# States of eleven chunks on ScalarE in eight scaled pieces, sums merged across tiles, Sin tables first, and a new order: one core of a Trainium2 chip

## The chip, the cores and the metric

The kernel runs on one core of one Trainium2 chip. The time is that of one execution on the device, in microseconds (us). A core has five engines that run side by side, each through its own list of instructions in order: TensorE (PE; its weight loads are shown apart as PEld), VectorE (DVE), ScalarE (ACT), GpSimd (POOL) and SyncE (SP), which here only issues transfers. One engine waits for another by semaphores.

## The reference

Two layers in a row, batch 4, 768 positions (S), 8 heads of 48 columns (D), 384 columns together (C). The first is a linear attention with a state that decays:

```python
for t in range(S):
    cur = np.einsum('bhd,bhe->bhde', u[None] * kt, vt)
    y[:, :, t] = np.einsum('bhd,bhde->bhe', rt, state + cur)
    state = wt[:, :, :, None] * state + np.einsum('bhd,bhe->bhde', kt, vt)
```

The second takes the 384 columns of y, projects them to three parts and gates them:

```python
proj = x @ w_proj
x1, x2, x3 = (proj[..., :D].copy(), proj[..., D:2 * D].copy(), proj[..., 2 * D:].copy())
X2 = np.fft.rfft(x2, n=S, axis=1)
H = np.fft.rfft(filter_fft, n=S, axis=0)[None, :, :]
x2_conv = np.fft.irfft(X2 * H, n=S, axis=1)
y = x1 * x2_conv * x3
return (y @ w_out).astype(np.float32)
```

Inputs and output are float32.

## The kernel before, in words

**Attention.** The 768 positions are cut into 6 chunks of 128, so that the 4 batches have 24 chunks, numbered through. For a chunk SP loads w, k, r and v (ldw, ldk, ldr, ldv; 192 KB each, six buffers of each). ACT takes the logarithm of w (lw). PE multiplies it by triangular masks, which gives the sums of logarithms up to each position (cs, and ce without the position itself; ce's last 8 columns are the sums over the whole chunk). ACT's exponentials of these (en or enp, eq) scale k and r (kh or khp, q or qp, on POOL or DVE), PE transposes both (tqk), ACT or DVE copies the result to SBUF (tT), and PE forms the scores (sc), which are masked on DVE (mt), or copied by ACT and masked on POOL (ma, mm). The state is carried by kv on PE: the state of the chunk before, taken in through an identity, plus k times v. Then S scales it by the chunk's decay: in the kernel before that is one VectorE product for every chunk (L610). The output of a chunk is y (or yb, where PE also adds the bonus term vc through an identity; with y, xn on DVE adds it). The bonus needs the row sums of r k u (rk, rku, cc, then vc on POOL). yt transposes y, xT copies it.

**Gate.** After the third chunk of a batch, sums and differences of mirrored chunks are formed (sa, sb) and folded once more (fp, fm), which shortens the Fourier sums. x2 projects them, ab copies, f is the forward transform in six slots, da and db multiply by the filter's transform (UA, UB), pp adds both (P), i1 and i2 are the inverse transform, s and d combine their sum and difference (SD), p1 and p3 are the other two projections (x1, and g or gc with gm), yy multiplies everything, po is the output product, o its copy, st the store. At the end of batch 3 the inverse transform and the gates run in halves (i1h, ech, sh, dh, yyh).

**Start.** POOL makes index ramps and masks, DVE makes angles (ang), ACT takes their sines (F, the transform matrix). The filter is loaded whole (filt, 1152 KB), folded to a sum and a difference (fs, fd: L399, L402), transformed by hf and turned into factors by ht, hr, hb, he.

**What sets the order.** A string, ORDER, written out by hand or by a program, holds one word for each step: the engine's letter (P, V, A, G, S), the step's name, its chunk or batch, and after @ the PSUM bank. Every engine issues its words in that sequence; a "!" makes a POOL step wait for the DVE step of certain kinds that stands last ahead of it. Banks 0 to 5 hold one tile at a time, so that a word with a bank waits until the bank's last reader is done. Each step is a function `op_<name>`; L237 is the line of every copy by ACT, L238 of those by DVE and POOL.

Of the kernel before, what the change touches and what calls it, by code (L numbers as in the profile page):

```python
# [10 lines left out]
FP32 = mybir.dt.float32  # L11
BF16 = mybir.dt.bfloat16
# [25 lines left out]
V:mem1 V:mem3 G:mkd! G:mke! G:iota! V:mem0 A:tLn G:mki! S:ldw1 S:ldu S:ldw0 A:lw1 V:mem4 V:mem2  # L38
A:lw0 G:iorot! P:zs29@0 V:ang2 S:ldr0 S:ldk0 S:ldk1 S:ldw2 S:ldr1 P:cs1@0 A:en1 V:ang1 V:ang0 V:mem7
A:uc0 P:cs0@1 A:en0 S:ldfilt P:ce1@2 S:ldv0 S:ldw3 V:rk0 A:eq1 G:rk1! V:mem5 V:angn G:kh0! P:us0@0  # L40
G:q1! S:ldr2 P:ce0@3 A:uv0 A:sin V:rku0 V:kh1 V:rku1 V:cc0 P:mtr0@0 A:eq0 A:lw2 P:tqk1@2 V:cc1 V:fs
A:tT1 P:ce2@3 P:cs2@1 P:mtr2@4 A:eq2 P:hf0@2 A:mc0 V:q0 V:rsc S:ldk2 A:v0 A:lw3 V:fd G:rk2! G:q2!
A:ht0.1 A:mc2 A:ht0.0 S:ldv1 A:enp2 P:hf1@3 P:tqk0@5 V:mem6 V:ms0 A:tT0 P:kv0@0 V:hr0.1 V:ms2
V:hr0.0 V:S0 P:hf2@2 V:khp2 P:sc0@8 A:he P:cs3@0 A:ht1.1 S:ldk3 S:ldw4 P:tqk2@1 A:ht1.0 V:rku2
G:vc0! G:v1! P:ce3@3 P:hf3@5 S:ldr3 S:ldv2 V:mt0 V:cc2 V:hr1.1 P:yb0@2 A:eq3 P:sc1@8 V:hr1.0 G:vc1!
S:ldw5 A:enp3 A:lw4 S:ldv3 V:mt1 A:tT2 A:v2 A:xc0 G:rk3! G:rku3! P:kv1@3 P:hf4@4 P:cs4@5 G:vc2! V:S1
V:khp3 A:enp4 A:ht2.0 P:yb1@1 P:yt0@2 G:v3! G:q3! P:kv2@3 S:ldk4 S:ldr4 V:cc3 S:ldr5 A:lw5 A:ht2.1
S:ldk5 G:rk4! G:vc3! P:ce4@0 P:sc2@8 P:ce5@4 A:xT0 A:xc1 A:eq5 V:S2 S:ldv4 P:hf5@3 P:tqk3@2 A:eqp4
# [5 lines left out]
P:yt5@1 P:ce7@5 V:sa4 P:x20.0.1@3 V:khp6 A:xT5 A:eq7 V:sb4 P:tqk6@4 V:sa5 A:ab0.0.1 P:x20.1.1@5
V:sb5 V:fp0.0 A:xT3 S:ldr7 A:v6 V:fm0.1 P:x20.0.0@3 P:x20.1.2@2 V:rku6 V:fm0.0 V:fp0.1 S:ldw8 G:q7!
P:x20.0.2@1 S:ldk7 A:ab0.0.0 S:ldp0 A:ab0.1.2 A:ab0.1.1 V:tT6 A:ab0.0.2 S:ldw10 V:cc6 P:f0.0@3
G:kh7! A:xT4 S:ldk8 P:kv6@2 P:x20.1.0@4 V:da0.0 G:vc6! A:ab0.1.0 A:lw8 P:f0.3@1 A:hb2 V:S6 G:rk7!
P:sc6@8 S:ldr8 P:f0.2@4 P:f0.4@2 A:wc0 P:ce8@3 P:tqk7@0 A:eq8 V:db0.1 A:tT7 S:ldw9 P:f0.5@1 P:cs8@5
V:da0.1 V:da0.2 G:rku7! P:p10.2.1@4 V:mt6 G:pp0.1! P:p10.0.1@3 P:p10.2.0@2 A:x10.2.1 S:ldv7 V:db0.2
# [48 lines left out]
A:tT21 G:kh22! V:db2.0 G:kh23! G:v21! A:eqp23 P:f2.5@1 V:qp23 A:ab2.0.0 V:db2.2 P:yb19@2 P:sc21@8
# [844 lines left out]
```

## Time and profile before

| | |
|---|---|
| median of 3 runs | 151.19 us (150.94 to 152.24) |
| the profiled execution | 150.74 us |
| its span, first to last instruction | 148.9 us |
| PE, DVE, ACT, POOL busy | 134.0, 134.8, 130.7, 108.8 us |
| mean granted clock of TensorE | 0.951 of full speed |
| transfers | 27.40 MB in 105702 packets, mean 184 GB/s |

The profile is that of one execution. Busy time is the union of an engine's instructions; neighbours on an engine overlap a little, so the time from one start to the next is shorter than a duration. A row of a timeline has start, duration, engine, line, operation, output and inputs, shape and count, and in brackets the idle time ahead of it with what ended it. A row of a table of stretches has the stretch, its length, then busy time and count for each engine, the granted clock, the share of the transfer engines and GB/s. The chain is the sequence of work that ended last, followed back from the last instruction.

### The profile page before, as it was taken

What the parts mean: (1) busy time and instruction counts of PE and PEld (TensorE: products, weight loads), DVE (VectorE), ACT (ScalarE), POOL (GpSimd) and SP (SyncE); (2) the same over time, 40 slices, a digit from 0 to 9 for tenths busy, and PEclk for the clock granted to TensorE, in tenths of its full rate; (3) what the DMA queues carried; (4) which work ended last, traced back from release to release, by engine and by line L of the source; (5) the groups of instructions that cost most, each with busy time, mean ns of one, the idle gap of its engine ahead of it and who ended that gap; (6) DMA issues with size and microseconds to landing.
All of it is one profiled execution on the core that took longest, in us unless ns stands there. A gap on an engine that the chain in (4) does not pass through costs nothing.

```text
span 148.9 us, 4080 instructions
## 1 busy us (share of the span) xinstructions
PE 134.0 (90%) x1499; PEld 89.9 (60%) x1499; DVE 134.8 (91%) x278; ACT 130.7 (88%) x274; POOL 108.8 (73%) x133
## 2 busy tenths in 40 slices
PE   6625699898999899999999999999999999999990
PEld 6423365666655567777666757666666776555840
DVE  6534999999999999999999999999999999999950
ACT  3799699999999899999999999999999975768470
POOL 7034179995579799999659999695599995846530
PEclk9955559999999999999999999999999999999998
DMA  4998999999999999989999999989980046001854
GB/s 80 212 278 218 181 210 187 219 188 243 178 258 201 263 203 183 217 167 214 227 232 200 222 204 194 198 168 219 229 186 0 4 173 254 0 0 53 314 210 170
DMA packets 105702, 27.40 MB, mean 184 GB/s; under 512 B 100305, under 2 KB 105682, under 8 KB 105682
## 3 DMA queue, kind: packets, MB, share of 16 engines
q1 hardware_dynamic: 105682, 27.14, 81.1%
q8 instruction: 11, 0.18, 0.5%
q14 instruction: 9, 0.07, 0.1%
HBM read 22.41 MB, written 4.72 MB: 182 GB/s over the span
## 4 chain that ended last, share of the span: by engine, by line
PE 68%; DMA 12%; SPq 5%; POOL 4%; DVE 4%; issue 3%; ACT 1%; ACTq 0%; DVEq 0%; POOLq 0%
PE p L688 14%; PE po L852 8%; PE i L773 6%; PE x L719 6%; PE tqk L561 6%; DMA filt<-in_moe_filter_fft_dram 5%; SPq L464 5%; PE sc L574 4%; DMA ldv<-in_v_dram 4%; DMA ldk<-in_k_dram 3%; PE f L739 3%; PE y L627 2%; PE yt L650 2%; PE cs L474 2%; PE kv L602 2%
## 5 line engine op out<-in xcount | busy, mean ns | idle before, releaser
L535 POOL TENSOR_TENSOR rk<-ldr,ldk 128x384 bf16<-128x384 f32 x23 | 23.0, 1003 | 11.1 <-DMA ldr<-in_r_dram 5.6
L688 PE MATMUL p<-xT,wproj 128*128 128x384 bf16 x144 | 28.8, 326 | 0.0
L555 POOL TENSOR_TENSOR vc<-v,cc 128x384 bf16<-128x384 bf16 x24 | 19.9, 831 | 10.5 <-PE sc L574 3.1
L581 DVE TENSOR_TENSOR mt<-sc,mask_excl 128x1024 bf16<-128x1024 f32 x21 | 25.4, 1210 | 0.1
L237 ACT ACTIVATE qkT<-tqk 128x1024 bf16<-128x1024 bf16 x22 | 22.7, 1031 | 0.7 <-PE tqk L561 0.5
L532 POOL TENSOR_TENSOR qk<-ldr,eq 128x384 bf16<-128x384 f32 x20 | 20.1, 1007 | 3.3 <-DVE rku L538 1.8
L561 PE MATMUL tqk<-ident,qk 128*128 128x128 bf16 x192 | 16.2, 228 | 2.6 <-POOL qk L532 1.8
L688 PEld LDWEIGHTS <-wproj 128*128 128x128 bf16 x144 | 13.0, 97 | 7.4 <-ACT wproj L237 0.3
L561 PEld LDWEIGHTS <-qk 128*128 128x128 bf16 x192 | 12.7, 102 | 5.5 <-POOL qk L532 2.2
L470 ACT ACTIVATE lg<-ldw 128x384 bf16<-128x384 f32 x24 | 12.6, 532 | 2.8 <-DMA ldw<-in_w_dram 2.8
L852 PE MATMUL po<-wout,y 128*128 128x384 bf16 x72 | 14.4, 326 | 0.0
L237 ACT ACTIVATE x<-p 128x384 bf16<-128x384 f32 x24 | 11.7, 505 | 1.5 <-PE p L688 1.5
L237 ACT ACTIVATE ab<-x 128x384 bf16<-128x384 f32 x24 | 11.7, 501 | 1.1 <-PE x L719 0.8
L538 POOL TENSOR_TENSOR rku<-rk,u_bc 128x384 bf16<-128x384 bf16 x13 | 11.8, 913 | 0.4
L541 DVE TENSOR_REDUCE cc<-rku 128x8 f32<-128x384 bf16 x22 | 11.7, 537 | 0.0
L499 ACT ACTIVATE eq<-ce 128x392 f32<-128x392 f32 (+1 forms) x21 | 10.6, 514 | 0.6 <-PE ce L486 0.3
L764 DVE TENSOR_TENSOR UB<-f,T 128x768 bf16<-128x768 f32 x12 | 11.1, 943 | 0.0
L237 ACT ACTIVATE v<-ldv 128x384 bf16<-128x384 f32 x20 | 10.8, 548 | 0.3 <-DMA ldv<-in_v_dram 0.2
L237 ACT ACTIVATE xT<-yt 128x384 bf16<-128x384 bf16 x22 | 10.8, 503 | 0.2
L610 DVE TENSOR_TENSOR S<-kv,eq 128x384 bf16<-128x384 f32 x20 | 10.9, 543 | 0.0
L528 POOL TENSOR_TENSOR qk<-ldk,en 128x384 bf16<-128x384 f32 x10 | 10.0, 1003 | 0.8 <-DMA ldk<-in_k_dram 0.8
L761 DVE TENSOR_TENSOR UA<-f,T 128x768 bf16<-128x768 f32 x11 | 10.3, 943 | 0.1
(152 smaller groups left out, 372.9 us busy)
## 6 DMA issues: line engine op xcount, KB each, us to landing
ldw<-in_w_dram SPq DMA_DIRECT2D x24, 192.0 KB, 3.8
ldr<-in_r_dram SPq DMA_DIRECT2D x24, 192.0 KB, 4.2
ldk<-in_k_dram SPq DMA_DIRECT2D x24, 192.0 KB, 3.7
ldv<-in_v_dram SPq DMA_DIRECT2D x24, 192.0 KB, 3.8
out_dram<-o SPq DMA_DIRECT2D x12, 192.0 KB, 2.3
out_dram<-filt SPq DMA_DIRECT2D x12, 192.0 KB, 2.2
o<-in_moe_w_proj_dram SPq DMA_DIRECT2D x3, 576.0 KB, 6.0
filt<-in_moe_filter_fft_dram SPq DMA_DIRECT2D x1, 1152.0 KB, 8.0
```

Source lines behind the costliest of these rows:

```text
L237: return nc.scalar.activation(out=o, in_=i, func=AF.Copy)
L470: nc.scalar.activation(out=lg_b[c % 3][:, :, 0:D], in_=ld["w"][c % LD], func=AF.Ln)
L532: return two(e).tensor_mul(qk_b[c % 3][:, 0, :, 0:D], ld["r"][c % LD], eq)
L535: return two(e).tensor_mul(rk_b[c % 2], ld["r"][c % LD], ld["k"][c % LD])
L538: return two(e).tensor_mul(rku_b[c % 2], rk_b[c % 2], u_bc)
L541: nc.vector.tensor_reduce(out=cc_b[c % 3], in_=rku_b[c % 2], axis=AX.X, op=ALU.add)
L555: return two(e).tensor_mul(vc_b[c % 3], v_b[c % 4], cc_b[c % 3].to_broadcast([L, H, D]))
L561: nc.tensor.transpose(p[:, x, j, :], qk_b[c % 3][:, x, 2 * j:2 * j + 2, :], ident)
L581: nc.vector.tensor_mul(mt_b[c % 3], bank_of[f"sc{c}"].rearrange("p q j t -> p (q j) t"), dataclasses.replace(m[:, :], ap=[m[:, :].ap[0], [ ...
L688: nc.tensor.matmul(p, wproj[:, n, cb, fb * L:(fb + 1) * L], xT_b[b % 2][:, NT * hf:NT * hf + NT, cb, :], start=(cb == 0), stop=(cb == CB - 1),
L764: nc.vector.tensor_mul(UB[:, n], twice(bank_of[f"f.{b}.{2 * n + 1}"][:, :]), t2(n, 1))
L852: nc.tensor.matmul(p, y_b[0][:, cb, ti * L:(ti + 1) * L], wout[:, cb, :], start=(cb == FIRST[0]), stop=(cb == FIRST[-1]),)
```

## The change

**States.** `op_S` gets a second form. Where the word's engine is A, ScalarE makes a chunk's state in eight pieces of 128x48, one for each of the 4 pairs of heads and each head of a pair, since one ACT instruction takes one scale for a partition:

```diff
     def op_S(e, c):
         ph = eq_b[c % 3][:, C:].rearrange("p (a b) -> p a b", b=2)
+        if e == "A":
+            for j in range(HP):
+                for i in (0, 1):
+                    nc.scalar.activation(
+                        out=S_b[nth(c)][:, j, i], in_=bank_of[f"kv{c}"][:, j, i], func=AF.Copy,
+                        scale=ph[:, j, i:i + 1],
+                    )
+            return
         nc.vector.tensor_mul(
             S_b[nth(c)], bank_of[f"kv{c}"], ph.to_broadcast([L, HP, 2, D])
         )
```

The words are A:S0, S1, S2, S4, S7, S8, S9, S10, S15, S19 and S22; the other nine states stay on V.

**Merged steps.** The tiles sd, fo and SD become one tile each, so that one instruction covers what two or three did:

```diff
+    def op_fpm(e, b):
+        return two(e).tensor_add(fo[:, :, 0], sd[:, :, 0], sd[:, :, 2])
+
+    def op_fmm(e, b):
+        return two(e).tensor_sub(fo[:, :, 1], sd[:, :, 0], sd[:, :, 2])
...
+    def op_ppm(e, b):
+        return two(e).tensor_add(P_b[b % 2], UA, UB)
...
+    def op_yym(e, b):
+        return two(e).tensor_mul(y_b[0], SD, g_b[b % 2])
```

fpm and fmm (two 384-wide halves each) take the place of all 16 fp and fm, ppm (2304 wide) of pp in batches 0 and 1, yym (2304 wide) of yy in batches 0 to 2. In batch 3 the last half of one gate is cut in two (yyq).

**Sin first.** The tables for Sin are loaded ahead of everything, the angles follow, then the sines as steps of their own, then the tables for the logarithm and exponential; before, those of the logarithm were first, and Sin lay between:

```diff
-    def op_sin(e, k_):
-        for ti in range(NT):
-            nc.scalar.activation(
-                out=F[:, ti, :], in_=low[:, ti * S:(ti + 1) * S], func=AF.Sin,
-                scale=TWO_PI / UNIT,
-            )
+    def op_tS(e, k_):
+        nc.scalar.preload_act_table(AF.Sin)
...
+    def op_sn(e, ti):
+        nc.scalar.activation(
+            out=F[:, ti, :], in_=low[:, ti * S:(ti + 1) * S], func=AF.Sin,
+            scale=TWO_PI / UNIT,
+        )
```

**Small new steps.** hm, um and uw prepare a tile uh that no step of the new order reads (a mask on POOL, three 8-wide products on PE, one small product on DVE); z2 is two warming products of 512 columns. Further functions (rt, rT, cu, cv, gg, ic, dg and others) are defined and not called.

**Order.** All of ORDER is new. By its words the engines also trade other steps: v leaves ACT for POOL and DVE (20 to 16 on ACT), copies xT go from ACT to DVE (2 to 7 on DVE), the copies of y on ACT go from 15 to 11 (one of them, xr, gets its bonus on POOL by xg), the sums xn on DVE from 9 to 13 and the bonus products on PE (yb) from 15 to 10, three sign copies (ms) go from DVE to ACT, fs goes from DVE to POOL, gc on ACT rises from 6 to 8 and X from 1 to 4. Two lines of it, old and new:

```diff
-V:mem1 V:mem3 G:mkd! G:mke! G:iota! V:mem0 A:tLn G:mki! S:ldw1 S:ldu S:ldw0 A:lw1 V:mem4 V:mem2
+S:ldw1 V:mem1 G:iota0! V:mem7 V:mem0 G:mki! G:mke! G:hm0! G:mkd! S:ldu V:mem5 S:ldw2 A:tS0 S:ldv0
...
```

Three places of the instruction lists show it. First ACT from the program's start; lg is the logarithm of w, cs and en the exponential for k, eq that for r, F the sines. Before:

```order
L342 ACT_TABLE_LOAD
L470 ACTIVATE lg_104<-ldw_80 128x8x48
L470 ACTIVATE lg_103<-ldw_79 128x8x48
L492 ACTIVATE en_110<-cs_267 128x384
L237 ACTIVATE u_top<-u_row 1x384
L492 ACTIVATE en_109<-cs_276 128x384
L499 ACTIVATE eq_113<-ce_280 128x392
L237 ACTIVATE u_bc<-us 128x384
L346 ACT_TABLE_LOAD
L346 ACTIVATE F<-o_170 128x768 x3
L350 ACTIVATE rot<-rang 128x12
L351 ACT_TABLE_LOAD
```

and now:

```order
L362 ACT_TABLE_LOAD
L240 ACTIVATE u_top<-u_row 1x384
L368 ACTIVATE F<-o_171 128x768 x2
L374 ACTIVATE rot<-rang 128x12
L368 ACTIVATE F<-o_171 128x768
L365 ACT_TABLE_LOAD
L493 ACTIVATE lg_105<-ldw_81 128x8x48
L240 ACTIVATE u_bc<-us 128x384
L493 ACTIVATE lg_103<-ldw_79 128x8x48
L493 ACTIVATE lg_104<-ldw_80 128x8x48
L240 ACTIVATE m_b<-mtr_295 128x2x192
L417 ACTIVATE m_b<-mtr_295 128x2x192
```

then, three exponentials further on, the state of chunk 0 (S from kv, eight pieces) up to the logarithm for chunk 4:

```order
L522 ACTIVATE eq_112<-ce_314 128x392
L529 ACTIVATE cs_326<-cs_326 128x384
L648 ACTIVATE S_137<-kv_344,eq_112 128x48 x8
L522 ACTIVATE eq_114<-ce_331 128x392
L493 ACTIVATE lg_104<-ldw_83 128x8x48
```

Two table loads stand where three stood, the sines stand ahead of the first logarithm instead of behind two, and the state of chunk 0 stands between the exponentials of chunks 0 and 2.

Second POOL, around the filter's folded sum (UA from filt, 1152 wide); vc is the bonus term of chunk 0, q and rk those of chunks 2 and 1. In the list before no such row exists on POOL. Now:

```order
L561 TENSOR_TENSOR rku_117<-rk_115,u_bc 128x384
L555 TENSOR_TENSOR qk_106<-ldr_91,eq_112 128x8x48
L590 TENSOR_TENSOR vc_128<-v_121,cc_125 128x384
L422 TENSOR_TENSOR UA<-filt 128x1152
L555 TENSOR_TENSOR qk_108<-ldr_93,eq_114 128x8x48
L558 TENSOR_TENSOR rk_115<-ldr_93,ldk_87 128x384
L558 TENSOR_TENSOR rk_116<-ldr_92,ldk_86 128x384
```

The sum moved here from DVE, ahead of q of chunk 2 and rk of chunks 2 and 1.

Third ACT in the stretch of chunks 7 to 11, in the middle of the program; qkT is the transposed q and k, xT the transposed y, x the first projection, eq, en, cs and ce exponentials, lg logarithms. Before:

```order
L492 ACTIVATE en_110<-cs_1122 128x384
L237 ACTIVATE qkT_131<-tqk_1124 128x1024
L510 ACTIVATE ce_1148<-ce_1148 128x384
L237 ACTIVATE xT_144<-yt_1144 128x384
L470 ACTIVATE lg_103<-ldw_79 128x8x48
L237 ACTIVATE xT_144<-yt_1167 128x384
L492 ACTIVATE en_111<-cs_1175 128x384
L237 ACTIVATE v_122<-ldv_100 128x384
L237 ACTIVATE qkT_132<-tqk_1188 128x1024
L237 ACTIVATE x_147<-p_1_0_0_1206 128x384
L237 ACTIVATE x_147<-p_1_1_0_1211 128x384
L237 ACTIVATE v_123<-ldv_101 128x384
```

and now:

```order
L240 ACTIVATE qkT_131<-tqk_1135 128x1024
L648 ACTIVATE S_138<-kv_1127,eq_114 128x48 x8
L522 ACTIVATE eq_113<-ce_1144 128x392
L493 ACTIVATE lg_105<-ldw_84 128x8x48
L240 ACTIVATE v_122<-ldv_100 128x384
L240 ACTIVATE xT_144<-yt_1202 128x384
L493 ACTIVATE lg_103<-ldw_79 128x8x48
L515 ACTIVATE en_111<-cs_1222 128x384
L240 ACTIVATE qkT_132<-tqk_1238 128x1024
L533 ACTIVATE ce_1230<-ce_1230 128x384
L648 ACTIVATE S_139<-kv_1256,eq_112 128x48 x8
L240 ACTIVATE v_123<-ldv_101 128x384
```

The states of chunks 8 and 9 (S from kv), eight pieces each, now stand between the copies and exponentials of the same stretch; before, each was one DVE row.

More of the change, by code (lines that the diff above doesn't have):

```diff
@@ L37 @@
 ORDER = """
-V:mem1 V:mem3 G:mkd! G:mke! G:iota! V:mem0 A:tLn G:mki! S:ldw1 S:ldu S:ldw0 A:lw1 V:mem4 V:mem2
[L39 to L48, printed above, removed]
@@ L54 @@
[L54 to L59, printed above, removed]
@@ new lines @@
+G:iorot0! V:ang2 A:uc0 V:ang0 V:mem4 S:ldr0 A:sn2 A:sn0 A:sr0 V:mem2 V:mem3 V:ang1 S:ldw0 A:sn1
+S:ldk0 S:ldv1 A:tLn0 P:us0@0 P:zs29@1 S:ldk1 A:lw2 A:uv0 A:lw0 P:cs2@1 A:lw1 P:mtr2@2 P:ce1@0
+P:cs1@3 S:ldfilt S:ldw4 V:v1 A:mc2 A:ms2 P:ce0@2 A:enp2 A:enp1 A:eq0 G:v0! G:rk0! P:cs0@4 G:rku0!
+A:enp0 V:cc0 P:ce2@5 V:khp0 V:khp1 G:q0! G:vc0! S:ldk2 S:ldr2 P:kv0@4 A:S0 A:eq2 G:fs! V:fd S:ldw3
+V:rsc V:khp2 S:ldr1 P:tqk0@2 P:um0@3 S:ldv2 P:z2@4 P:hf0@4 P:hf1@5 A:lw4 A:eqp1 A:tT0 A:ph1 A:lw3
+P:ce3@1 A:ht0.0 V:uw0 V:qp1 P:sc0@8 G:q2! P:tqk1@0 S:ldw5 G:rk2! S:ldk3 S:ldk4 A:ht0.1 S:ldk5
@@ L325, in op_uv, with op_hm, op_um, op_uw @@
         copy(e, u_bc.rearrange("p h d -> p (h d)"), bank_of["us"])
+    def op_hm(e, k_):
+        nc.gpsimd.memset(hm, 1.0)
+        for lo, m in ((0, 1), (D - 1, -1)):
+            nc.gpsimd.affine_select(
+                out=hm, in_=hm, pattern=[[m * L, CB], [-m * D, H]], base=lo,
+                channel_multiplier=m, compare_op=ALU.is_ge, fill=0.0,
+            )
+    def op_um(e, k_, bank):
+        p = ps("um", bank, (L, CB, H))
+        for cb in range(CB):
+            nc.tensor.matmul(
+                p[:, cb, :], u_top[:, cb * L:(cb + 1) * L], mask_incl[:, 0:H],
+                start=True, stop=True,
+            )
+    def op_uw(e, k_):
+        nc.vector.tensor_mul(uh, bank_of["um"], hm)
     def op_ang(e, ti):
@@ L541, in op_cc, with op_rt, op_rT, op_cu @@
         nc.vector.tensor_reduce(out=cc_b[c % 3], in_=rku_b[c % 2], axis=AX.X, op=ALU.add)
-    def op_rh(e, c):
-        x = rku_b[c % 2]
-        return two(e).tensor_add(rh_b[c % 2], x[:, :, 0:D // 2], x[:, :, D // 2:])
-    def op_ch(e, c):
-        nc.vector.tensor_reduce(out=cc_b[c % 3], in_=rh_b[c % 2], axis=AX.X, op=ALU.add)
+    def op_rt(e, c, bank):
+        p = ps(f"rt{c}", bank, (L, CB, L), BF16)
+        f = rk_b[c % 2].rearrange("p h d -> p (h d)")
+        for cb in range(CB):
+            nc.tensor.transpose(p[:, cb, :], f[:, cb * L:(cb + 1) * L], ident)
+    def op_rT(e, c):
+        copy(e, rT_b[c % 2], bank_of[f"rt{c}"])
+    def op_cu(e, c, bank):
+        p = ps(f"cu{c}", bank, (L, H))
+        for cb in range(CB):
+            nc.tensor.matmul(
+                p, rT_b[c % 2][:, cb, :], uh[:, cb, :], start=(cb == 0), stop=(cb == CB - 1)
+            )
+    def op_cv(e, c):
+        copy(e, cc_b[c % 3], bank_of[f"cu{c}"])
     def op_v(e, c):
@@ L645, in op_xc, with op_xr, op_xg @@
         copy(e, xn_b[c % 3], bank_of[f"y{c}"].rearrange("p h d -> p (h d)"))
+    def op_xr(e, c):
+        op_xc(e, c)
+    def op_xg(e, c):
+        x = xn_b[c % 3]
+        return two(e).tensor_add(x, x, vc_b[c % 3].rearrange("p h d -> p (h d)"))
     def op_yt(e, c, bank):
@@ L706, in op_g, with op_gg @@
         )
+    def op_gg(e, b, fb, hf):
+        nc.vector.tensor_mul(
+            g_b[b % 2][:, fb, halves[hf]], bank_of[f"p3.{b}.{fb}.{hf}"],
+            bank_of[f"p1.{b}.{fb}.{hf}"],
+        )
     def op_gc(e, b, fb, hf):
```

223 lines of the change are left out of this document (128 added, 95 removed).

## The prediction

> **What bounds the kernel now.** I read the page first, then the table of stretches, then the chain that ended last, and the timeline of ScalarE (ACT) last, because the change loads that engine.
>
> ```profile
> span 148.9 us, 4080 instructions
> PE 134.0 (90%) x1499; PEld 89.9 (60%) x1499; DVE 134.8 (91%) x278; ACT 130.7 (88%) x274; POOL 108.8 (73%) x133
> ```
>
> Three engines are near 90%, and such a share does not say which of them sets the end. I cut the span at 23.6 us (start), at 50, and at 118.1, where ACT has copied the last chunk's transposed q and k (tT23).
>
> ```profile
> core 0: us, PE busy (x) PEld busy (x) DVE busy (x) ACT busy (x) POOL busy (x), PEclk, DMA share, GB/s
> 0.00:23.60 23.60, 15.30 (x137) 10.42 (x137) 15.63 (x47) 18.70 (x33) 10.43 (x27) 0.71 0.88 194
> 23.60:50.00 26.40, 23.87 (x316) 16.04 (x310) 26.02 (x48) 25.64 (x56) 22.20 (x25) 1.00 1.02 221
> 50.00:118.10 68.10, 68.10 (x826) 46.25 (x827) 68.02 (x132) 67.10 (x143) 58.47 (x66) 1.00 0.91 185
> 118.10:149.00 30.90, 26.75 (x231) 17.18 (x228) 25.11 (x54) 19.27 (x46) 17.66 (x18) 0.98 0.38 141
> ```
>
> From 50 to 118 PE never idles, DVE idles 0.1 us and ACT 1.0 us: all three are full, and only POOL has room. PE's idle time lies before 50 us. ACT's lies in the start (4.9 us) and behind 118 us. So work that is added to ACT before 118 us has almost no gap to fall into. The chain shows what hangs on that point.
>
> ```profile
> 6.81 7.97 DMA filt<-in_moe_filter_fft_dram
> 14.80 1.37 DVE UA L399
> 16.22 2.10 PE hf L416 x6
> ...
> 119.44 0.33 PE sc L574 x8
> ...
> 142.53 1.69 PE po L852 x9
> 144.22 0.02 issue
> ```
>
> In the start PE waits for the filter and for its folded sum. At the end PE runs without a gap from the last chunk's scores (sc23, 119.44) to its last output product (144.22); copy and store then take 4.7 us to the span's end. Outside the span the execution has 150.74 - 148.9 = 1.84 us.
>
> **What an ACT entry costs.** Neighbours overlap, so I count from one start to the next, not the duration.
>
> ```profile
> 26.18 0.53 ACT L470 ACTIVATE lg<-ldw 128x384 bf16<-128x384 f32 x1
> 26.59 0.59 ACT L434 ACTIVATE E<-hf,rot 128x384 f32<-128x384 f32 x1
> 27.05 0.51 ACT L237 ACTIVATE xT<-yt 128x384 bf16<-128x384 bf16 x1
> 27.43 0.52 ACT L237 ACTIVATE xn<-y 128x384 bf16<-128x384 f32 x1
> ...
> 32.77 0.17 ACT L513 ACTIVATE eq<-ce 128x8 f32<-128x8 f32 x1
> 32.83 1.02 ACT L237 ACTIVATE qkT<-tqk 128x1024 bf16<-128x1024 bf16 x1
> ```
>
> A plain 384-wide copy steps by 0.37 us (27.05 to 27.43), one that loads w or v by 0.41, the 8-wide exponential by 0.06, so a plain entry is 0.053 us plus 0.83 ns a column. E, whose scale is a column of numbers in memory, one per partition, steps by 0.46: that kind of scale costs 0.09 more. It isn't hidden behind a neighbour of the same kind:
>
> ```profile
> 21.06 1.02 ACT L434 ACTIVATE E<-hf,rot 128x384 f32<-128x384 f32 x2
> ...
> 115.88 1.04 ACT L237 ACTIVATE qkT<-tqk 128x1024 bf16<-128x1024 bf16 x1
> 116.78 0.52 ACT L237 ACTIVATE xT<-yt 128x384 bf16<-128x384 bf16 x1
> 117.16 1.07 ACT L237 ACTIVATE qkT<-tqk 128x1024 bf16<-128x1024 bf16 x1
> 118.06 0.98 ACT L237 ACTIVATE v<-ldv 128x384 bf16<-128x384 f32 x2
> ```
>
> Two such E span 1.02 us, a step of 0.45 and one duration of 0.57. The 1024-wide copy steps by 0.90; tT23 ends its turn at 118.1.
>
> **The states (S) on ACT.** No row shows a 48-wide scaled piece. Below, it steps like the 8-wide row with 40 columns more: 0.093 us. Above, nothing overlaps: E's duration of 0.575 less 336 columns, 0.295. I take 0.053 + 0.04 + 0.087 = 0.18, since E is the nearest row; a state is then 8 x 0.18 = 1.44 us (0.74 to 2.36), where DVE needed a step of 0.47 (duration below). [...]
>
> ```profile
> L610 DVE TENSOR_TENSOR S<-kv,eq 128x384 bf16<-128x384 f32 x20 | 10.9, 543 | 0.0
> 92.88 1.48 DVE L767 TENSOR_TENSOR P<-UA,UB 128x768 bf16<-128x768 bf16 x3
> 96.35 0.34 DVE L665 TENSOR_TENSOR sd<-xT,yt 128x384 bf16<-128x384 bf16 x1
> 96.61 0.34 DVE L668 TENSOR_TENSOR sd<-xT,yt 128x384 bf16<-128x384 bf16 x1
> L535 POOL TENSOR_TENSOR rk<-ldr,ldk 128x384 bf16<-128x384 f32 x23 | 23.0, 1003 | 11.1 <-DMA ldr<-in_r_dram 5.6 <-DVE sgn L315 5.5
> ```
>
> ACT up to tT23, old list against new: ten states +14.4; three sign copies (ms) +1.3; one more output copy +0.4; three v (0.41), four xT, four xn and one g (0.37 each) fewer, -4.6; one scaled E fewer -0.5; one table load fewer -1.28 (row below). Together **+9.7 us**. By the same steps the old list up to there is 106.8 us of work, so 118.1 held 11.3 us of waiting: 4.9 visible in the start, 1.8 visible later, 4.6 in slacks that the overlap of durations hides. The new list is 116.5 us.
>
> **The merged operations.** On DVE a 384-wide bf16 pair steps by 0.26 (96.35 to 96.61), a 768-wide one by 0.47 (92.88: three in 1.48, the last one with its whole duration of 0.54). So 2304 wide is some 1.27, and a merge saves about 0.06 (folded sums) to 0.14 (product sums, gates): 1 us in all. With eleven states gone (-5.2) and copies xT, sums xn added, DVE's whole list is an estimated 4 us shorter. That buys nothing by itself while PE and ACT are full. It costs a batch's first gate a later start, by the 0.9 us of the other two; other groups that stand ahead of the output products in PE's queue hide that, and uncovered it is 0.9 us a batch.
>
> **Start.** Sin first saves a load:
>
> ```profile
> 3.57 0.52 ACT L470 ACTIVATE lg<-ldw 128x384 bf16<-128x384 f32 x1 [1.49 <-DMA ldw<-in_w_dram]
> ...
> 7.61 1.28 ACT L346 ACT_TABLE_LOAD   x1
> 8.90 2.31 ACT L346 ACTIVATE F<-o 128x768 bf16<-128x768 int16 x3
> ...
> 15.40 0.52 ACT L237 ACTIVATE v<-ldv 128x384 bf16<-128x384 f32 x1 [0.17 <-DMA ldv<-in_v_dram]
> 16.20 0.52 ACT L470 ACTIVATE lg<-ldw 128x384 bf16<-128x384 f32 x1 [0.28 <-DMA ldw<-in_w_dram]
> ```
>
> [...]
>
> Loads land in the order of issue, 0.8 to 0.9 us apart behind the filter (15.40, 16.20). The new order issues nine loads ahead of the filter instead of eight: it lands at 14.8 + 0.9 = 15.7. The folded sum that PE needs first moves from DVE (1.37) to POOL: at 1.0 us for 384 columns (the rk row above) some 2.9 for 1152, with 1.4 (DVE's own time) and 3.0 as bounds. Behind it on POOL wait q2, rk2 and rk1. The first filter product then starts at **18.6 instead of 16.2**, and behind it in PE's queue stand ce3, sc0, tqk1, cs4, and so all of chunks 0 and 1. ACT in its new order waits 0.8 to begin; 1.2 for u; 1.2 for the first kv (enp0, khp0, kv0, S0 follow each other with nothing between; eq2 and w of chunk 4 stand behind S0); 1.9 for w of chunk 4, now the first load behind the filter (16.5); 0.8 for w of chunk 3, the fourth behind it; 0.8 for the filter product and ce3. That is 6.7 us by 22 us, and it eats what the saved load gave.
>
> **The sum.** ACT reaches the end of tT23 after 116.5 + 6.7 + later waiting. For that I keep the 1.8 us that the table shows from 23.6 to 118.1 (bounds 0, when ACT is always the last, and 6.4, with the hidden slacks as before). So 125.0 instead of 118.1. PE reached sc23 1.3 us after tT23; now it waits and starts at 125.1. Behind it the new order leaves PE two p3 products (0.49 each) and one f (0.33) less and one kv (0.33) more: 24.8 - 1.0 = 23.8. Then 4.7 to the end: span 153.6, and with 1.84 the execution is **155.4 us** against 150.74 for the profiled one, whose median of runs is 151.19.
>
> **Rivals.**
>
> *Faster: the pieces overlap.* At 0.093 the ten states cost 7.0 us less, ACT reaches tT23 at 118.0 as before, and PE alone decides. For it: an 8-wide entry really took 0.06. Against: the pair of E. PE's time would change by +1.9 (filter later, less 0.5 of work put ahead), -3.0 (18 loads behind the filter, batch 0 is complete at 15.7 + 18 x 0.9 = 31.9, while its v of chunk 5 now lands at 34.9, a wait on the chain; row below), -0.4 (five identity products of 0.16 fewer, two warming ones more) and -1.2 (half of PE's idle 2.5 in 23.6 to 50, by the lighter DVE): -2.7, or **148.0 us**; the clock, 0.71 of full speed in the start, is taken as before.
>
> ```profile
> 29.61 5.25 DMA ldv<-in_v_dram
> ```
>
> *No change.* PE is full from 50 us on with the same work, the pieces cost around 0.11, and the later filter uses up the earlier loads: 150.74 - 0.4 + 0.4 = **150.7 us**. This is also the case in which the change moves load between engines without moving the bound.
>
> *Dearer pieces.* If half of the 0.11 overlap is lost for so short an entry, a piece is 0.237, a state 1.90, ten of them 4.6 us more: **160.0 us**. [...]
>
> **How the numbers follow.** ACT full, pieces at about 0.18: 0.60. Dearer: 0.10. No change: 0.17. Faster: 0.13. About 1% either way is what a measurement of this kernel can tell from no change, so slower 0.70, same 0.17, faster 0.13. The forecast's own range is 152.0 (pieces of 0.16, no later waiting) to 159.0 (later waiting of 5.4). Downward I widen it to 149.5 to take in the case without a change, so that some 0.11 is left out below and 0.05 above.
>
> **What would show it.** Right: 88 ACT rows of 128x48, 0.18 us from start to start; ACT without idle from 25 to 125 us while PE, and DVE too, show idle there, at sc and yt waiting for ACT's copies; the first filter product near 18.6; tT23's end near 125; 23.8 us of PE behind sc23. Wrong: pieces that step by 0.1 or less, ACT with free time before 118 us, or PE full from 45 us on, which would mean the start decided.

## The result, and the profile after

The changed kernel takes **159.90 us** (median of 4 runs, 159.60 to 160.18) where the kernel before took 151.56 beside it (4 runs, 150.94 to 152.24): ratio 1.055 (95% interval 1.049 to 1.061). Slower, as forecast, but 4.5 us more so than the 155.4 forecast, and 0.9 above the range's end. The profiled execution took 159.82, its span is 158.1. Now and then an execution takes 1.5% or more longer than the fastest of its kernel; the medians of the experiments, and all ratios, leave such executions out, and the profiles of kernels 2 and 13 are of such ones.

The page of the changed kernel, its span and busy times:

```profile
span 158.1 us, 4149 instructions
PE 136.0 (86%) x1499; PEld 90.2 (57%) x1499; DVE 134.4 (85%) x264; ACT 141.1 (89%) x355; POOL 109.8 (69%) x135
```

ACT has 10.4 us more than before, DVE is level, and the shares say little. The table of stretches says more:

```profile
core 0: us, PE busy (x) PEld busy (x) DVE busy (x) ACT busy (x) POOL busy (x), PEclk, DMA share, GB/s
0.00:23.60 23.60, 13.66 (x114) 9.72 (x115) 13.57 (x42) 16.94 (x37) 14.72 (x30) 1.00 0.92 200
23.60:50.00 26.40, 22.58 (x302) 14.99 (x300) 23.85 (x43) 26.23 (x72) 21.50 (x25) 1.00 0.93 195
50.00:118.10 68.10, 64.83 (x765) 42.98 (x763) 65.05 (x116) 67.65 (x175) 53.79 (x61) 1.00 0.91 187
118.10:158.10 40.00, 34.97 (x329) 22.56 (x324) 31.93 (x66) 30.31 (x75) 19.75 (x21) 0.97 0.35 119
```

From 23.6 to 118.1 ACT idles 0.6 us in all (26.40 - 26.23 and 68.10 - 67.65), PE 7.1 and DVE 5.6. Before, PE idled 2.5 there, all of it ahead of 50 us. The engine that never stops has changed from PE to ACT. A state on ACT, that of chunk 1, in ACT's timeline:

```profile
25.00 0.46 ACT L515 ACTIVATE en<-cs 128x384 f32<-128x384 f32 x1
25.37 1.59 ACT L648 ACTIVATE S<-kv,eq 128x48 bf16<-128x48 f32 x8
26.84 0.51 ACT L417 ACTIVATE m_b<-mtr 128x384 bf16<-128x384 bf16 x1
```

From 25.37 to 26.84 are 1.47 us, 0.184 a piece: forecast 1.44 and 0.18. The start, in the chain that ended last:

```profile
7.48 7.59 DMA filt<-in_moe_filter_fft_dram
15.14 3.79 POOL UA L422
18.98 2.09 PE hf L439 x6
```

The filter lands at 15.07 (forecast 15.7), but POOL's folded sum takes 3.79 us (forecast 2.9), so the first filter product starts at 18.98 (forecast 18.6). Six of them take 2.09 us, half speed (0.31 us from start to start, where a 384-wide product later takes 0.16), as the six before the change did. And the turn of the last chunk's copy, in ACT's timeline:

```profile
126.13 0.52 ACT L240 ACTIVATE v<-ldv 128x384 bf16<-128x384 f32 x1
126.68 1.02 ACT L240 ACTIVATE qkT<-tqk 128x1024 bf16<-128x1024 bf16 x1
127.60 0.87 ACT L240 ACTIVATE filt<-po 128x384 f32<-128x384 f32 x2
```

tT23 ends its turn at 127.6, where 118.1 stood before and 125.0 was forecast. Behind it, the chain isn't PE alone any more:

```profile
128.43 0.33 PE sc L609 x8
128.76 0.61 PE p L744 x3
...
129.39 0.35 ACT x L240
...
129.78 1.65 ACT S L648 x8
...
131.48 0.33 PE y L665 x4
...
150.17 2.06 DMA out_dram<-filt
...
153.24 0.66 PE po L945 x3
```

The chain leaves PE at 129.4 for a copy and the state of chunk 22 and is back 2.1 us later, at y; near the end it goes through a store, since the copy that frees the bank of the last products goes into the buffer that this store still reads. PE has other products to do meanwhile. Its own timeline shows what of this is idle time, 0.45 and 0.29 us:

```profile
131.48 0.33 PE L665 MATMUL y<-S,qkT 128*128 128x96 bf16 x4 [0.45 <-ACT S L648]
...
153.24 0.81 PE L945 MATMUL po<-wout,y 128*128 128x384 bf16 x4 [0.29 <-ACT filt L240]
```

### The profile page after: what moved, and what is told of

Its sections match the earlier page's. It is cut to its first block, busy times and chain, and to the rows that moved or that the text cites. A ratio compares the mean times of both kernels' runs of the same rounds, so it can differ in the third digit from the quotient of the medians.

```text
span 158.1 us, 4149 instructions
## 1 busy us (share of the span) xinstructions
PE 136.0 (86%) x1499; PEld 90.2 (57%) x1499; DVE 134.4 (85%) x264; ACT 141.1 (89%) x355; POOL 109.8 (69%) x135
## 3 DMA queue, kind: packets, MB, share of 16 engines
q1 hardware_dynamic: 105682, 27.14, 76.7%
## 4 chain that ended last, share of the span: by engine, by line
ACT 43%; PE 32%; DMA 6%; issue 4%; SPq 4%; POOL 4%; DVE 3%; ACTq 1%; DVEq 0%
ACT S L648 9%; ACT qkT L240 7%; PE p L744 6%; PE x L781 5%; DMA filt<-in_moe_filter_fft_dram 5%; SPq L487 4%; PE po L945 3%; ACT lg L493 3%; ACT x L240 3%; ACT eq L522 3%; PE f L801 3%; ACT xn L240 3%; POOL UA L422 2%; ACT v L240 2%; ACT xT L240 2%
## 5 line engine op out<-in xcount | busy, mean ns | idle before, releaser
L616 DVE TENSOR_TENSOR mt<-sc,mask_excl 128x1024 bf16<-128x1024 f32 x21 | 25.5, 1215 | 0.3 <-PE sc L609 0.3
L240 ACT ACTIVATE qkT<-tqk 128x1024 bf16<-128x1024 bf16 x22 | 24.0, 1092 | 0.2
L558 POOL TENSOR_TENSOR rk<-ldr,ldk 128x384 bf16<-128x384 f32 x22 | 21.9, 1000 | 0.0
L648 ACT ACTIVATE S<-kv,eq 128x48 bf16<-128x48 f32 x88 | 18.8, 391 | 2.1 <-PE kv L637 2.1
L551 POOL TENSOR_TENSOR qk<-ldk,en 128x384 bf16<-128x384 f32 x12 | 12.0, 1001 | 6.9 <-ACT qkT L240 4.9
L493 ACT ACTIVATE lg<-ldw 128x384 bf16<-128x384 f32 x24 | 14.4, 617 | 0.4 <-DMA ldw<-in_w_dram 0.4
L240 ACT ACTIVATE x<-p 128x384 bf16<-128x384 f32 x24 | 13.1, 567 | 0.8 <-PE p L744 0.5
L561 POOL TENSOR_TENSOR rku<-rk,u_bc 128x384 bf16<-128x384 bf16 x11 | 10.1, 914 | 2.9 <-DVE rku L561 1.6
L838 PE MATMUL i<-m_b,P 128*128 128x384 bf16 x54 | 10.8, 326 | 0.5 <-ACT S L648 0.5
L609 PE MATMUL sc<-qkT 48*128 48x128 bf16 x192 | 9.7, 222 | 0.6 <-ACT qkT L240 0.6
L760 DVE TENSOR_TENSOR g<-p,x 128x384 bf16<-128x384 f32 x16 | 8.6, 550 | 1.5 <-ACT x L240 1.5
```

The costliest lines, as they stand in the source:

```text
L240: return nc.scalar.activation(out=o, in_=i, func=AF.Copy)
L493: nc.scalar.activation(out=lg_b[c % 3][:, :, 0:D], in_=ld["w"][c % LD], func=AF.Ln)
L558: return two(e).tensor_mul(rk_b[c % 2], ld["r"][c % LD], ld["k"][c % LD])
L616: nc.vector.tensor_mul(mt_b[c % 3], bank_of[f"sc{c}"].rearrange("p q j t -> p (q j) t"), dataclasses.replace(m[:, :], ap=[m[:, :].ap[0], [ ...
L648: nc.scalar.activation(out=S_b[nth(c)][:, j, i], in_=bank_of[f"kv{c}"][:, j, i], func=AF.Copy, scale=ph[:, j, i:i + 1],)
```

## The experiments

Two theories at first. A: the pieces' price on ACT sets the time. B: the new order itself does. One table for all kernels; sc6, sc12 and sc23 are the starts of PE's first score product of chunks 6, 12 and 23 in the profiled execution, read from PE's rows, and "behind" is the span less sc23.

| kernel | median us | ratio to before (95%) | sc6 | sc12 | sc23 | behind |
|---|---|---|---|---|---|---|
| before | 150.7 to 151.6 | 1 | 42.8 | 70.5 | 119.4 | 29.5 |
| changed | 159.90 | 1.055 (1.049 to 1.061) | 44.0 | 77.7 | 128.4 | 29.7 |
| 1 states back on DVE | 158.85 | 1.053 (1.046 to 1.060) | 43.6 | 76.8 | 126.2 | 30.2 |
| 2 states on ACT, old order | 172.59 | 1.144 (1.131 to 1.156) | 52.4 | 87.1 | 139.4 | 33.2 |
| 3 constant scale | 153.37 | 1.017 (1.009 to 1.024) | 42.1 | 72.8 | 122.1 | 29.2 |
| 4 stores early | 159.02 | 1.055 (1.046 to 1.063) | 43.5 | 77.1 | 127.8 | 29.3 |
| 5 folded sum on DVE | 159.22 | 1.055 (1.048 to 1.063) | 43.1 | 76.7 | 127.4 | 30.2 |
| 6 = 3 + 4 + 5 | 153.16 | 1.014 (1.007 to 1.022) | 40.4 | 72.1 | 121.4 | 29.4 |
| 7 = 1 + 4 + 5 | 155.72 | 1.031 (1.020 to 1.043) | 42.9 | 76.1 | 125.5 | 29.2 |
| 8 as 7, six states on ACT | 156.67 | 1.039 (1.030 to 1.048) | 42.4 | 74.8 | 124.8 | 29.3 |
| 9 merges alone, old order | 150.58 | 1.001 (0.996 to 1.006) | 41.3 | 68.8 | 117.9 | 30.0 |
| 10 three states, old order | 155.87 | 1.033 (1.025 to 1.040) | 41.9 | 76.5 | 125.3 | 29.3 |
| 11 as 7, copies to ACT | 158.44 | 1.049 (1.043 to 1.056) | 42.4 | 77.0 | 126.5 | 29.4 |
| 12 filter first, old order | 155.44 | 1.032 (1.024 to 1.039) | 47.7 | 74.7 | 123.6 | 29.4 |
| 13 warming products, old order | 151.03 | 0.999 (0.995 to 1.003) | 43.2 | 72.5 | 122.1 | 29.5 |
| 14 = 9 + 13 | 151.73 | 1.007 (1.003 to 1.010) | 42.1 | 70.1 | 119.9 | 30.6 |

All but kernel 2 need 29.2 to 30.6 us behind sc23 and 48.8 to 50.7 from sc12 to sc23: the times part mostly ahead of chunk 12. The changed kernel is 1.2 us late at sc6, 7.2 at sc12 and 9.0 at sc23. A profiled execution can lie 0.5 to 2.3 us off its kernel's median (those of 9, 11 and 12 lie below it, those of 2 and 13 above), so that differences of half a us between two rows of one column carry nothing.

**1 and 2: the states moved across.** In 1 the eleven words change engine in the new order, in 2 in the old one (with the new form of `op_S`).

```diff
1 -A:S0 ... A:S22
  +V:S0 ... V:S22
2 -V:S0 ... V:S22
  +A:S0 ... A:S22
```

> The changed kernel with all eleven states back on DVE as one product each, everything else as changed. Theory A (ACT is the bound up to the last chunk's transposed copy, by the states' eight pieces of 0.18 us): ACT is 16 us shorter, DVE 5 us longer, PE sets the pace again, 150.5 us (148.5 to 152.5). Rival B (the new order's later start and its end cost the time, whichever engine makes the states): 157 to 160 us.

> The kernel before, in its own order, with the same eleven states made on ACT in eight scaled pieces and nothing else changed. Theory A: 16.2 us more on an engine with some 5 to 7 us of waiting to give up before the last chunk, so 158 to 162 us, and PE and DVE with idle time from 50 to 118 us. Rival B: the states are hidden, 150 to 153 us.

Measured: 158.85 and 172.59. Theory A as stated falls: without the pieces the new order is hardly faster, and in the old order its 158 to 162 is missed by more than 10 us. Theory B fails too: in the old order the pieces cost 21.5 us, about 2 for each state. The stretches of kernel 1 from 23.6 to 118.1, and the last part of the second by itself:

```profile
23.60:50.00 26.40, 22.71 (x302) 15.06 (x300) 25.09 (x46) 22.33 (x49) 21.66 (x26) 1.00 0.99 208
50.00:118.10 68.10, 66.64 (x783) 44.10 (x782) 67.34 (x122) 62.45 (x131) 54.50 (x62) 1.00 0.90 187
77.00:118.10 41.10, 41.08 (x483) 27.15 (x477) 41.10 (x74) 39.99 (x86) 32.07 (x38) 1.00 0.84 176
```

ACT now has 9.7 us free, and DVE carries what ACT gave up (137.9 us busy in all): it idles 2.1 us where it idled 0.5 before the change, and PE waits 5.2. Up to 77 us no engine is full, and the lists wait for each other: up to sc12 PE idles 15.4 us, against 10.8 in the kernel before. From 77 us on PE and DVE are full, so PE does set the pace again there, as theory A has it, but from a point that it reaches 6.3 us late. In kernel 2, busy tenths and granted clock on its page:

```profile
PE   6427794696899977975999997799979949999990
...
PEclk9955798589579999998799999999999996999999
```

The clock drops in mid-program, in or behind stretches in which PE idles. After one of them, 1.95 us up to 43.8, products step at half speed until 49.8: the eight of a tqk span 1.06 us instead of 0.62, and the granted clock from 23.6 to 50 is 0.74. So here a late state costs PE's waiting first and slower products next.

**3: the price of the pieces.** Same words, same 88 pieces, but a constant in place of the column of decays (the decay is left out in the eleven states, so the output isn't the reference's).

```diff
-                        scale=ph[:, j, i:i + 1],
+                        scale=0.25,
```

> The changed kernel with a constant 0.25 as the scale of the eleven states on ACT, so that the chunk's decay is left out there and the count of pieces stays at 88. Theory A, with 0.09 us of each 0.18 being the scale that is read from memory: pieces step by 0.09 to 0.10, a state takes 0.75 to 0.80, ACT has 7.5 us less, 152.5 us (151 to 154.5). If the price lies in the number of instructions and not in the scale: pieces still step by 0.18 and the time stays at 159 to 160. Rival B: 158 to 160 as well, with pieces of either length.

Measured: 153.37, as A expects. ACT's timeline and the group of kernel 3, the group of the changed kernel, and a stretch of kernel 3:

```profile
25.31 0.93 ACT L648 ACTIVATE S<-kv 128x48 bf16<-128x48 f32 x8
26.03 0.59 ACT L417 ACTIVATE m_b<-mtr 128x384 bf16<-128x384 bf16 x1
...
L648 ACT ACTIVATE S<-kv 128x48 bf16<-128x48 f32 x88 | 10.7, 301 | 2.0 <-PE kv L637 2.0
```

```profile
L648 ACT ACTIVATE S<-kv,eq 128x48 bf16<-128x48 f32 x88 | 18.8, 391 | 2.1 <-PE kv L637 2.1
```

```profile
50.00:118.10 68.10, 68.10 (x820) 46.19 (x817) 67.47 (x123) 67.62 (x184) 56.64 (x64) 1.00 0.95 198
```

A state steps by 0.72, a piece by 0.090: to 0.003 the sum of the plain entry's terms (0.053 + 0.04) in the prediction. The scale from memory adds 0.094 to every piece, 80 of which stand ahead of tT23: 7.5 us of ACT, of which 6.5 come out at the end. That is the largest part of the loss. No wait goes with the scale, since ACT makes the decays itself, ahead in its list. And PE is full again from 50 to 118.1, as before the change.

**4 and 5: the store and the folded sum.**

```diff
4 +S:st1.2 S:st1.4 S:st1.0 (behind S:st0.4, from their later places)
5 -G:fs! V:fd
  +V:fs V:fd
```

> The changed kernel with the stores of tiles 0, 2 and 4 of batch 1 issued right behind those of tiles 5 and 4 of batch 0 instead of at the end, so that the copies of batch 3, which write the same buffer, need not wait for them. If the store that stands on the chain (2.06 us) is worth what the prediction's tail lacked: 1.0 to 2.0 us less than the changed kernel, 158 to 159. If the tail hangs on something else: 159.5 to 160.2.

> The changed kernel with the filter's folded sum (fs) on VectorE ahead of the difference, as in the kernel before; nothing else changed. Theory A: the start is a cost of its own. POOL's sum took 3.8 us and held a 12-element VectorE product for 2.6 us; with fs on VectorE (1.4 us) the first filter product starts at about 16.6 instead of 19.0 and the end comes 1 to 2.4 us earlier: 157.5 to 159.0 us. Theory B: ScalarE's list up to the last chunk's copy sets the end whatever the start does, since its waits at the start are for loads and for k times v: then 159.3 to 160.2 us, as the changed kernel.

Measured: 159.02 and 159.22, with ratios equal to the changed kernel's; both lie between the ranges of their two theories. Kernel 4's chain no longer has the store, but DVE's gates of batch 3 in its place; its 0.9 us isn't told apart from nothing. In kernel 5 the first filter product starts 2.1 us earlier (16.91) and sc23 1.0 us earlier, in one profile, and the median is 0.22 above theory A's range and 0.08 below theory B's: nearer to B. While ACT is full, neither wait is worth more than these 0.7 to 0.9 us, if that.

**6, 7, 8: the same repairs, with ACT relieved.** 6 is 3 with both repairs, 7 is 1 with both; in 8 five states go to DVE and six stay on ACT.

```diff
6 -scale=ph[:, j, i:i + 1]          7 -A:S0 ... A:S22    8 -A:S1 A:S4 A:S8 A:S10 A:S19
  +scale=0.25                         +V:S0 ... V:S22      +V:S1 V:S4 V:S8 V:S10 V:S19
 all: -G:fs! V:fd  +V:fs V:fd,  S:st1.2 S:st1.4 S:st1.0 behind S:st0.4
```

> The changed kernel with three things undone together: the scale of the eight pieces is the constant 0.25 (the decay is left out in the eleven states, so that the output isn't the reference's; still 88 pieces), fs on VectorE, and batch 1's last three stores issued behind batch 0's. Theory A: price of the pointer scale (6.5 us by the run with constant scale), start and store add up, and the new order then stands level with the kernel before: 150 to 152 us. Theory B: with ScalarE relieved, start and stores are hidden by something else of the new order: 152.8 to 153.9, as with the constant scale alone.

> The changed kernel with all eleven states back on VectorE (as in the run that had 158.9 us), fs on VectorE ahead of the difference and batch 1's last three stores behind batch 0's. Theory A: VectorE and TensorE are the bound there, and the start's 2.4 us and the store's 0.9 us come on top: 155.5 to 157 us. Theory B: the order of the words was made for states on ScalarE; in-order waits between VectorE, ScalarE and the loads set the time and swallow both: 158 to 159.3 us.

> The changed kernel with five of the eleven states (chunks 1, 4, 8, 10, 19) back on VectorE and six on ScalarE, fs on VectorE, stores as in the two runs before. Theory A: ScalarE was the bound in the changed kernel, VectorE with all states back; half way between neither is as full, and the time is less than at either end: 152.5 to 155.5 us. Theory B: what costs the time is not the load of the one or the other but the order itself: the same as with all states back and the same start and stores, within 1 us: 155.5 to 158.5 us.

Measured: 153.16, 155.72, 156.67. Kernel 6 misses theory A (150 to 152) and is as B expects: the repairs add nothing to the constant scale's gain that the intervals tell apart, and 1.4% remains in the order. By sc6 it is 2.4 us ahead of the kernel before, by sc12 1.6 behind. In 7 they do pay: 3.1 us against kernel 1 (in the profiles 0.7 up to sc23 and 1.0 behind it), inside A's range. Kernel 8 is no better than 7: no best point half way, as B expects. In kernel 8 PE idles 3.6 us from 24 to 50 and 1.4 from 50 to sc23, ACT and DVE a few us as well: it waits a little for both.

**9: the merges alone**, in the old order.

```diff
-V:fp0.0 V:fm0.1 ... V:fm0.0 V:fp0.1 ... G:pp0.1! V:pp0.0 V:pp0.2 ... V:yy0.0 V:yy0.2 V:yy0.1
+V:fpm0 V:fmm0 ... V:ppm0 ... V:yym0
```

> The kernel before with the merged operations alone (fpm and fmm, ppm in batches 0 and 1, yym in batches 0 to 2, on VectorE, each behind the last of the inputs that it needs), its order otherwise kept. Theory A (the prediction's step): they take some 1 us off VectorE's list, and POOL loses four small sums, but TensorE is full from 50 us on, so that nothing is gained: within 0.7 us of the kernel before, 151 to 152.3. Theory B: VectorE's and TensorE's lists are coupled so tightly that 1 us of VectorE is 1 us of the end: 150 to 150.8. Theory C: the later start of a batch's first gate and first product is not hidden: 152.5 to 154.

Measured: 150.58 beside 150.80 for the kernel before, ratio 1.001 (0.996 to 1.006), theory A: no gain. Their costs in the changed kernel are as worked out (2304 wide 1.35 by duration, 768 wide 0.55):

```profile
L934 DVE TENSOR_TENSOR y<-SD,g 128x2304 bf16<-128x2304 bf16 x3 | 4.1, 1354 | 0.1
...
L731 DVE TENSOR_TENSOR fo<-sd 128x768 bf16<-128x768 bf16 x4 | 2.2, 552 | 0.1
```

**10: three states on ACT in the old order.**

```diff
-V:S8 ... V:S9 ... V:S10
+A:S8 ... A:S9 ... A:S10
```

> The kernel before with three states on ScalarE in eight pieces (chunks 8, 9 and 10, in the stretch from 55 to 68 us, in which TensorE, VectorE and ScalarE are all full) and the old order. Theory A: each state adds its 1.47 us to a full ScalarE and nothing else: 3 x 1.47 less some 1 us of ScalarE's slack, so 154 to 156.5 us. Theory B: as with all eleven in the old order, where 21.5 us were lost, 2.0 us for a state, since each late state also leaves TensorE idle until its clock is halved: 157 to 159 us, with matmuls at half speed in mid-program.

Measured: 155.87, inside A's range; 5.1 us more than the 150.80 beside it for three states, 1.7 each. But B's mark is there too: in the middle one of these stretches PE idles 3.8 us and DVE 6.4, and matmuls step at half speed from 71.1 to 74.5 (granted clock 0.90 over the 17 us of the stretch).

```profile
50.00:58.00 8.00, 7.39 (x88) 4.90 (x87) 7.91 (x15) 7.83 (x22) 6.46 (x8) 1.00 1.00 197
58.00:75.00 17.00, 13.24 (x153) 9.22 (x153) 10.60 (x18) 14.78 (x42) 12.51 (x14) 0.90 0.99 205
75.00:118.00 43.00, 43.00 (x505) 28.57 (x504) 42.48 (x86) 42.74 (x93) 33.27 (x38) 1.00 0.85 173
```

ACT isn't full in that stretch either (14.78 of 17). The state is finished about a us later than on DVE (1.47 instead of 0.47), and in an order without slack what is queued behind it comes late in turn. So I read the cost of a moved state as its latency as well as its load; no run here separates the two, since cheap pieces were not tried in the old order.

**11: copies from DVE to ACT**, on top of 7. (In the bonus of chunks 6, 7 and 8 this kernel reads an older tile, since vc stands behind yb there; its output isn't the reference's.)

```diff
-V:xn4 V:xn6 V:xn7 V:xn8 V:xn10 V:xT5 V:xT6 V:xT8 V:xT9 V:xT14, P:y4 ...
+A:xc4 A:xc6 A:xc7 A:xc8 A:xc10 A:xT5 A:xT6 A:xT8 A:xT9 A:xT14, P:yb4 ...
```

> The run with all states on VectorE, its folded sum on VectorE and the stores early (156.0 us), and now five sums xn (chunks 4, 6, 7, 8, 10; TensorE adds their bonus through the identity instead, 0.16 us each) and five copies xT (5, 6, 8, 9, 14) handed from VectorE to ScalarE, which takes 3.7 us from VectorE and adds 3.7 us to ScalarE. Theory A: with the states back VectorE's list is the bound (138.0 us busy, 3.2 more than before), so the end follows it: 152.5 to 154 us. Theory B: the new order's waits and its start set the time, not VectorE's load: 155.5 to 157 us.

Measured: 158.44, slower than kernel 7 by 2.7, so neither: a lighter DVE list doesn't make kernel 7 faster, as theory A had it. From 23.6 to 50 in kernel 7, then in kernel 11:

```profile
23.60:50.00 26.40, 22.93 (x301) 14.94 (x297) 25.09 (x45) 22.18 (x47) 21.92 (x26) 1.00 0.99 210
```

```profile
23.60:50.00 26.40, 21.43 (x284) 14.04 (x282) 23.22 (x40) 22.06 (x47) 20.75 (x26) 1.00 0.99 207
```

DVE idles 3.2 us instead of 1.3, PE 5.0 instead of 3.5: DVE now waits 1.6 us for one of the copies xT that ACT makes late, and PE 1.1 for the folded sum of y (fo) that follows. The place of a step in an in-order list weighed more than the load.

**12: the filter first**, in the old order.

```diff
-S:ldk1 S:ldw2 S:ldr1 ... S:ldfilt
+S:ldk1 S:ldfilt S:ldw2 S:ldr1
```

> The kernel before with the filter's load issued two loads earlier (behind k of chunk 1, ahead of w of chunk 2 and r of chunk 1), nothing else changed. Theory A: the filter sets TensorE's start and the end of its half-speed phase; it lands 1.6 us earlier and the end moves by 0.5 to 1.5 us: 150 to 151. Theory B: r of chunk 1 and w of chunk 2 land some 7 us later, and ScalarE and VectorE, which stand in order, wait for them instead: 152.5 to 156 us.

Measured: 155.44. It doesn't answer its question: the ramp from which the angles are made lies in the filter's buffer (L219), so that the angles waited for the load and read it (the output isn't the reference's).

```profile
2.93 0.79 DVE L330 TENSOR_SCALAR o<-filt,tcol 128x384 int32<-128x384 f32 x2 [0.22 <-POOL filt L271]
11.35 1.41 DVE L330 TENSOR_SCALAR o<-filt,tcol 128x384 int32<-128x384 f32 x4 [7.63 <-DMA filt<-in_moe_filter_fft_dram]
```

Whether an earlier filter helps stays open. It does show how much a late start costs: sc6 comes 4.9 us later than before, and 4.2 of it are still there at sc23.

**13 and 14: warming products** in PE's idle time in the start, in the kernel before and in kernel 9.

```diff
+P:zs24@4 (behind P:ce0@3)  P:zs10@4 (behind P:tqk1@2)  P:zs10@5 (behind P:mtr2@4)
```

> The kernel before with 44 warming products of 128 columns put into the idle time of TensorE's start (24 behind ce of chunk 0, 10 behind tqk of chunk 1, 10 ahead of the first filter product), nothing else changed. Theory A: TensorE's matmuls step at half speed from 8.0 to 21.6 us because it idles 2.7, 1.3 and 1.3 us there; kept busy it is at full speed by the first filter product (16.2 us), and up to 5 us of half-speed work take half the time: 149 to 150.6 us. Theory B: the half-speed phase has a length of its own, or the start is bound by loads and by VectorE's and ScalarE's work on the filter, and the products are in the way at best: 151 to 153 us.

> The kernel before with the merged operations alone, as in the run that showed no difference, and the same 44 warming products. Theory A: full speed early gives the same gain as without the merges, 148.8 to 150.6 us, and VectorE's shorter list may add a little where the start isn't TensorE's; this would be the version to keep. Theory B: neither helps, 151 to 153 us.

Measured: ratios 0.999 and 1.007, theory B. The half-speed phase ends at 18.4 us in 13 and at 17.3 in 14 instead of 21.6, in one profile each, but the end doesn't follow it. That the products brought the full speed isn't shown: in kernel 9 the phase ends at 17.6 without any warming. No kernel tried beats the kernel before.

## Why the prediction was wrong in size, step by step

ACT as the bound was right, but four terms of the sum came out too small: the later waiting on ACT, the start, the step from tT23 to sc23, and PE's time behind sc23. The range (152.0 to 159.0) took its width from the pieces and the later waiting alone, so that misses in the other terms had no room in it.

- **ACT takes PE's place as the bound: right.** ACT idles 0.6 us from 23.6 to 118.1; kernel 3, which only makes ACT's pieces cheaper, gives back 6.5 of 8.3 us, and PE is full again there.
- **The piece at 0.18: right** (0.184), with its three terms, 0.053 + 0.04 + 0.087, measured as 0.090 and 0.094. The dearer piece of 0.237 didn't come; the 0.11 of overlap in it is the 8-wide row's duration of 0.17 less its step of 0.06.
- **ACT's list of 116.5 us up to tT23: right**, 116.8 by its steps. Together with the waits below, tT23 ended 2.6 us later than forecast.
- **The start: mis-sized by 0.6.** ACT waited 7.3 us by its steps instead of 6.7. That the two are near is luck. The 1.9 us for w of chunk 4 never came: ACT took it at 16.16 without a pause. In its place the first kv held ACT for 2.1 us instead of 1.2, and the filter product and ce3 for 1.5 instead of 0.8:

```profile
14.30 1.64 ACT L648 ACTIVATE S<-kv,eq 128x48 bf16<-128x48 f32 x8 [2.08 <-PE kv L637]
15.78 0.55 ACT L522 ACTIVATE eq<-ce 128x392 f32<-128x392 f32 x1
16.16 0.58 ACT L493 ACTIVATE lg<-ldw 128x384 bf16<-128x384 f32 x1
```

  POOL's folded sum, 3.79 instead of 2.9, is outside the bounds that I gave (1.4 to 3.0):

```profile
15.09 1.36 DVE L425 TENSOR_TENSOR UA<-filt 128x1152 bf16<-128x1152 f32 x1 [0.99 <-DMA filt<-in_moe_filter_fft_dram]
16.37 2.58 DVE L377 TENSOR_TENSOR rot<-rot,rsc 128x12 f32<-128x12 f32 x1
```

  This is DVE's timeline: the difference starts 0.05 us ahead of POOL's sum and takes its usual time (1.36, and 1.35 in the kernel before), and the 12-element product behind it, 0.17 us in the kernel before, lasts 2.58, until POOL's sum is done (18.93). I read that as DVE waiting for POOL. If POOL in turn had first waited for the difference (to 16.45), its own share would be an estimated 2.5 us, inside my bounds; no run shows the sum with DVE idle. In kernel 5 it is POOL's row that is longer: its 384-wide product, which starts at 17.46 beside DVE's difference (16.62 to 17.97), lasts 1.37 us instead of 0.99.
- **Later waiting of 1.8: mis-sized, 3.4.** Only 0.6 of it shows as idle time; the rest lies in slacks that the overlap of durations hides. The forecast counted such slacks in the old list (4.6 us) and put them at nothing in the new one. The bounds (0 to 6.4) held it. With the start it makes 2.2 of the 2.6 us.
- **PE waits for tT23 and starts sc23 at once: failed, 0.7 us.** sc23 started 0.8 us behind tT23's turn, not 0.1. PE didn't wait for tT23: from 119.2 to 131.0 it has no idle time, and it still had a po and a p3 to do ahead of sc23. What held PE back through ACT lies earlier, last at 117.6 (a state, 0.45 us) and 119.2 (a copy, 0.13).
- **PE without a gap behind sc23: failed, 1.2 us.** From sc23 to the end of PE's last product are 25.7 us, against 25.5 in the kernel before; the forecast took 1.0 off. PE idles 0.8 of it, which I had put at nothing: 0.45 for state 22 in eight pieces on ACT, 0.29 behind the store, 0.07 for a gate. PE is busy 24.9 us there instead of 25.5, so of the 1.0 us of work taken off 0.6 arrives. From PE's last product to the span's end it is 4.1 us in both. In all 2.6 + 0.7 + 1.2 = 4.5 us of span.
- **The rival with cheap pieces, 148.0: wrong by 5.** Kernel 3 is that case, at 153.4. Its sum gave 3.0 us for the earlier completion of batch 0; kernel 6 does stand 2.4 us ahead at sc6, and has lost it by sc12, with PE idle no more than 0.3 us from 50 to 118. Part of the lead was work not yet done: PE starts 357 matmuls ahead of sc6 instead of 369, and 355 instead of 335 from there to sc12, which takes 31.6 us instead of 27.7 with 0.4 of PE's idle time in both. By their usual steps at full speed the 20 are an estimated 2.6 of these 3.9 us. So "no change" wasn't reached even with pieces at 0.09.
- **Merges worth 1 us of DVE and nothing at the end: right at the end** (9). On DVE the merged groups of kernel 9 are 0.7 us shorter by their steps, with four small sums taken over from POOL.
- **DVE's list 4 us shorter: wrong, 0.4** (134.8 to 134.4). The product held up in the start is 2.4 of that; copies xT and sums xn, for which the sum left 2.2 together, add 1.4 and 2.2 by their steps. So DVE had nothing to hand on when the states went back to it (1).

What stays open: why the new order with cheap pieces keeps 1.4% (PE is not idle longer there than before; its matmuls from sc6 to sc12 take more time than their number accounts for), and what an earlier filter is worth.

## What to carry over

Count what an operation adds to the engine that will be full after the move, by its step from start to start and with its kind of scale; then ask who waits for its result, since in an order without slack a result that comes later can cost more than the load (1.7 to 2.0 us for a state in the old order, 1.5 of work). A part of a change undone inside the new order isn't the old kernel: the rest was arranged around it, and 1, 2 and 11 each came out on the side that the load alone would not give. And behind the bound, look for waits in the new words before taking work off, and let the range hold every term of the sum that can miss.

## What the runs showed of the hardware

- A scale read from memory costs a 48-wide ACT entry 0.094 us, also when eight of them stand back to back (0.184 against 0.090).
- A 12-element DVE product lasted 2.58 us beside POOL's 1152-wide sum, 0.96 beside POOL's 384-wide product (kernels 5 to 7), and 0.17 with POOL idle.
- In the table of stretches the start of the changed kernel (0 to 23.6 us) reads a granted clock of 1.00, and the first filter products in it step by 0.31 us, half speed (0.16 later). The matmul's own step tells.
